# Sliding-window attention followed by a GELU feed-forward, on one core: loading and first product in smaller pieces, the first attention in another order, joined stores in the tail, value loads behind a wait

## The chip, the cores and the metric

The kernel runs on one core of one Trainium2 chip. Its engines work side by side and meet at semaphores: TensorE (PE, with its weight loads listed as PEld), VectorE (DVE), ScalarE (ACT), GpSimd (POOL) and SyncE (SP). SP issues most loads; ACT and POOL issue some DMAs too. All DMAs run on 16 DMA engines. The metric is the device time in microseconds of one execution, less being better.

## The reference

Two stages are computed, the second on the output of the first. All inputs and the output are fp32.

```python
# q, k, v: (8, 8, 576, 64): batch, heads, sequence, head dimension
scores = (1 / sqrt(64)) * q @ k.transpose(0, 1, 3, 2)
mask   = abs(pos[:, None] - pos[None, :]) <= 32           # a band of 65 keys for each query
attn   = softmax(where(mask, scores, -1e9))
x      = (attn @ v).transpose(0, 2, 1, 3).reshape(4608, 512)

h   = x @ w_in                                            # (512, 2048)
g   = 0.5 * h * (1 + tanh(sqrt(2 / pi) * (h + 0.044715 * h**3)))
out = g @ w_out                                           # (2048, 512) -> (4608, 512)
```

## The kernel before

**Stages.** The 4608 tokens of the second stage are nine tiles of 512 (`t` = 0 to 8), those of attention eight batches of 576 (`b` = 0 to 7). Before the loop stands a start-up: load batch 0, attention of batch 0, load and cast of `w_in`, and the first product of tile 0. Then stage `t` multiplies tile `t` with `w_in` (`ffn_in`, L456), applies GELU on ACT (L464), and multiplies with `w_out` while the attention of batch `t` + 1 is woven in between the matmuls by a table written by hand (`PLAN`, `PLAN_0`: "s" scores, "m" mask, "v" weigh with the values, "x" spread into `xT`). Tile 0 uses plain matmuls for the second product (`ffn_out_0`, L525), the others a Winograd form of 7 half-size products (`ffn_out`, L551).

**The order.** Nothing is scheduled by a planner: each engine and each queue takes its instructions in the order of the program text. An instruction waits for what it reads and for the buffer that it writes, and everything behind it on its engine waits with it.

**Loads and casts.** SP's queue holds, in this order: batch 0's q, k, tails and v; `w_in` in four column blocks of 512 (`load_w_in`, L192; block 0 in two loads, the others in one each); batch 1's q and k (L136); `w_out` (L196) in four blocks, the last in two loads, with batch 1's values between them; batch 2's q and k (L165, L167). Weights arrive as fp32 in a pool of five staging buffers and are cast to fp16 by `cast_w` (L201), chunk by chunk of 128 rows. Block 0 and block 1 of `w_in` are cast by POOL alone, the later blocks by DVE (chunks 0 and 1) and POOL (2 and 3).

**First attention.** Batch 0 is handled in four pairs of heads. For each pair q and k are cast to fp16 (`cast_early`, L264), transposed by PE (`trans_pair`, L293 and L295), copied out of PSUM by DVE (`trans_out`: QT at L300, KT at L301), multiplied to scores (`score`, L360), exponentiated on ACT (L370), masked by the band on DVE (`mask`, L376), weighed with the values (`weigh`: sums at L389, values at L395), inverted on ACT (`invert`, L408 and L409), and spread into `xT` by DVE (`spread`, L418). The values of a pair are cast by POOL (`cast_v`, L274) and then copied to a shifted place by DVE (`pair_v`, L182 and L183). `spin` (L227) issues PE work that nobody reads, to fill PE's waiting time. The tails are the last 64 positions of the sequence.

**Later batches.** From batch 2 on, q and k are cast by DVE (L321, L329) and transposed by DMA from SP's queue (`cast_and_turn`: QT at L324, KT in two halves at L331, KL at L336). Values are loaded as fp16 by POOL's queue (`load_v`: four loads at L175, a fifth at L177), each batch one stage ahead. In stage `t` ≥ 1 the loads of batch `t` + 2 stand in POOL's queue right where the plan weighs the tail of the batch before (`v-1`), ahead of that stage's stores; the loads of batch 2 stand earlier, in the first product of stage 1, behind a one-column POOL copy (L727) that waits for a GELU. The pair copies of V are two DMAs on SP at the end of the stage.

**Stores.** `store` (L515) writes 128 rows of a tile. Rows lie in the order (position modulo 4, position), so the rows are cut where that order jumps; in a tail of a batch this gives runs of 24 rows (16 for batch 0). In the last tile the stores alternate between SP and ACT; in the others they are on POOL.

Of the kernel before, what the change touches and what calls it, by code (L numbers as in the profile page):

```python
# [64 lines left out]
def kernel(  # L65
# [9 lines left out]
    nc = tc.nc  # L75
# [5 lines left out]
    NT = NTOK // 512  # L81
# [25 lines left out]

    load_table(exp_set)


    idn = const.tile([128, 128], FP16, name="idn")
    full = const.tile([128, 4, 56], FP16, name="full")
    ones = const.tile([128, 64], FP16, name="ones")
# [74 lines left out]
    def stage_w():  # L188
        return stage.tile([128, 4, 512], FP32, name="wst", tag="stage")

    def load_w_in(i, w, c0=0, c1=4):
        nc.sync.dma_start(w[:, c0:c1, :], w_in_v[:, c0:c1, 512 * i:512 * i + 512])  # L192
        return w
# [2 lines left out]
        nc.sync.dma_start(w[:, c0:c1, :], w_out_v[:, 4 * i + c0:4 * i + c1, :])  # L196
        return w

    def cast_w(w, dst, on_dve=2, cs=range(4), on_act=()):
        for c in cs:  # L200
            (nc.scalar.copy if c in on_act else nc.vector.tensor_copy if c < on_dve else nc.gpsimd.tensor_copy)(  # L201
                dst[:, c, :], w[:, c, :])

    qk, tails, vs, vtail = load_early(0)
# [7 lines left out]
    vs(2, 3)  # L212
    vs(4, 5)
    vs(6, 7)
    wi = [load_w_in(0, stage_w(), 0, 2)]
    load_w_in(0, wi[0], 2, 4)
    wi[1:] = [load_w_in(i, stage_w()) for i in range(1, 4)]


    idle = KTs[1][:, 0, 0:512]  # L220
    nc.vector.memset(idle, 0.0)
# [33 lines left out]
    QTs = {}  # L255
# [40 lines left out]
        if now:  # L296
            trans_out(b, pr, pt)

    def trans_out(b, pr, pt):
        nc.vector.tensor_copy(QTs[b][:, pr, :, 0:128], pt[:, 0:4, :])  # L300
        nc.vector.tensor_copy(  # L301
            KTs[b % 2][:, pr, :].rearrange("d (p j) -> d p j", j=4),
            pt[:, 4:8, :].rearrange("d j p -> d p j"))
# [5 lines left out]
    def bank16(i):  # L309
        return psM.tile([128, 8, 128], FP16, name="pt", tag=f"x{i}")  # L310
# [190 lines left out]
    out_v = out.rearrange("(b p j) f -> b j p f", b=B, j=4)  # L501
    pys = {}

    turn_about = [nc.sync, nc.scalar]

    def store(t, t4, yo, cols=slice(0, 512), eng=None):
        m = 0
        while m < 128:
            b, c = divmod(t * 512 + t4 * 128 + m, S)
            q0, n = (0, cut(b)) if c < 4 * cut(b) else (cut(b), 144 - cut(b))  # L510
            j, p = divmod(c - 4 * q0, n)
            e = min(n - p, 128 - m)
            if t == NT - 1 and eng is None:
                turn_about.reverse()
            (eng or turn_about[0] if t == NT - 1 else eng or nc.gpsimd).dma_start(  # L515
                out_v[b, j, q0 + p:q0 + p + e, cols], yo[m:m + e, cols])
            m += e

    later, unpaired = [], []

# [13 lines left out]
    def ffn_out(t, i):  # L534

        n, blk, f = i // 16, i // 8 % 2, i % 8
        a, w, new = WINO[n]
        end = t == NT - 1
        if i % 16 == 0 and new:
            pys[n % 2] = bank((1 + n) % 2)  # L540
            if end and n == 4:
                pys["apart"] = psO.tile([128, 512], FP32, name="py2", tag="O")
        py = pys[n % 2].rearrange("p (b c) -> p b c", b=2)
        apart = end and blk and n in (4, 6)
        if a[0] == "A":
            r0, c0 = 8 * (int(a[2]) - 1) + f, 256 * (int(a[1]) - 1) + 128 * blk
            lhsT = gTs[t][:, r0, c0:c0 + 128]
        else:
            lhsT = wino[a][:, f, 128 * blk:128 * blk + 128]
        one = end and n in (4, 6)  # L550
        nc.tensor.matmul(pys["apart"][:, 0:256] if apart else py[:, blk, :], lhsT,  # L551
                         wino[w][:, f, :], start=(new and i % (8 if one else 16) == 0),
                         stop=(i % (8 if one else 16) == (7 if one else 15)),
                         skip_group_check=True)
        if i % 16 < 15:
            return
        yo, left, right = wino["yo"], slice(0, 256), slice(256, 512)
        C11, C12, C21, C22 = (yo[:, r:r + 2, c] for r in (0, 2) for c in (left, right))

        M1, U2, U3 = C21, C12, C22  # L560
        if n == 0:
            nc.vector.tensor_copy(M1, py)
        elif n == 1:
            nc.vector.tensor_tensor(U2, py, M1, op=ALU.add)
        elif n == 2:
            nc.vector.tensor_copy(C11, py)
            if end:
                for x in range(2):
                    store(t, x, yo[:, x, :], left, nc.sync)
        elif n == 3:  # L570
            nc.vector.tensor_tensor(U3, py, M1, op=ALU.add)
        elif n == 4:
            if not end:
                nc.vector.tensor_tensor(C22, py, U3, op=ALU.add)
            else:
                for x, part in enumerate((py[:, 0, :], pys["apart"][:, 0:256])):
                    nc.vector.tensor_tensor(C22[:, x, :], part, U3[:, x, :], op=ALU.add)
                    store(t, 2 + x, yo[:, 2 + x, :], right)
        elif n == 5:
            nc.vector.tensor_tensor(C21, py, M1, op=ALU.add)  # L580
            for x in range(2):
                store(t, 2 + x, yo[:, 2 + x, :], left if end else slice(0, 512))

    def ffn_last(t):
        py = pys[0].rearrange("p (b c) -> p b c", b=2)
        yo, right = wino["yo"], slice(256, 512)
        for x in range(2):
            part = pys["apart"][:, 0:256] if x and t == NT - 1 else py[:, x, :]
            nc.vector.tensor_tensor(yo[:, x, right], part, yo[:, x, right], op=ALU.add)
            if t < NT - 1:  # L590
                store(t, x, yo[:, x, :])
            else:
                store(t, x, yo[:, x, :], right, nc.scalar if x else nc.sync)


    cast_open(0)
    cast_early(0, 0, (nc.vector, nc.gpsimd))
    trans_pair(0, 0, bank16(0))
    cast_tails(0, nc.vector)
    spin(3, 512)  # L600
    trans_tails(0, bank16(1))
    both = (nc.gpsimd, nc.gpsimd)
    cast_early(0, 1, both)
    cast_early(0, 2, both)
    cast_v(0, 0)
    cast_early(0, 3, both)
    cast_v(0, 1)
    cast_v(0, 2)
    cast_v(0, 3)
    cast_w(wi[0], w_in16[:, :, 0:512], 0, (0, 1))  # L610
    cast_w(wi[0], w_in16[:, :, 0:512], 0, (2, 3))


    qk, tails, vs, vtail = load_early(1)
    for h in range(0, H, 2):
        qk(h)
    wo = [load_w_out(0, stage_w())]

    def turn(g):
        pt = bank16(0)  # L620
        trans_pair(0, g, pt, now=False)
        return pt

    def weighed(g):
        o, d = weigh(0, g, other=(g % 2 == 0))
        ods[g] = (o, invert(0, g, o, d))

    def paired(g):
# [1 line left out]

    ods = {}
    score(0, 0, 0)
    spin(2, 512, 1)
    pt = turn(1)
    trans_out(0, 1, pt)
    mask(0, 0)
    spin(4, 512, 1)
    score(0, 1, 1)
    pt = turn(2)
    trans_out(0, 2, pt)  # L640
    cast_vt(0)
    mask(0, 1)
    spin(4, 512, 0)
    score(0, 2, 0)
    paired(0)
    spin(3, 512, 1)
    weighed(0)
    mask(0, 2)
    pt = turn(3)
    trans_out(0, 3, pt)  # L650
    spread(0, 0, *ods[0])
    spin(4, 512, 1)
    score(0, 3, 1)
    paired(1)
    spin(2, 512, 0)
    weighed(1)
    paired(2)
    mask(0, 3)
    weighed(2)
    spread(0, 1, *ods[1])  # L660
    ffn_in(0, 0, 0, 2)
    paired(3)
    spread(0, 2, *ods[2])
    weighed(3)
    for fc in (1, 2, 3):
        ffn_in(0, fc, 0, 2)
    for fc in range(4):
        ffn_in(0, fc, 2, 3)
    cast_w(wi[1], w_in16[:, :, 512:1024], 0)
    for fc in (4, 5):  # L670
        ffn_in(0, fc, 0, 3)
    spread(0, 3, *ods[3])
    for c in (2, 3):
        cast_w(wi[c], w_in16[:, :, 512 * c:512 * c + 512])
    wo += [load_w_out(1, stage_w()), load_w_out(2, stage_w())]
# [35 lines left out]
    for t in range(NT):  # L711
# [28 lines left out]
        for i in range(113 if t else 65):  # L740
            for act in plan.get(i, "").split():
# [14 lines left out]
                elif kind == "t":  # L756
                    trans_tails(1, bank16(1))
                elif kind == "c":
                    if g == 1:
                        B12 = combine_w()  # L760
                    combine(g, nc.vector)
                elif kind == "s":
                    score(*group(g), at)
                elif kind == "d":
                    pair_v(b, nc.vector.tensor_copy, slice(2 * g, 2 * g + 2))
                elif kind == "m":
                    mask(*group(g))
                elif kind == "v":
                    bb, gg = group(g)
                    o, d = weigh(bb, gg, at)  # L770
                    ods[g] = (o, invert(bb, gg, o, d))
                    if t and g < 0 and b + 1 < B:
                        load_v(b + 1)
                        unpaired.append(b + 1)
                    if t and g == (3 if att else -1):
                        load_table(gelu_set)
                else:
                    spread(*group(g), *ods[g])
# [1 line left out]
                pair_v(2, nc.vector.tensor_copy, slice(i // 10, i // 10 + 4))  # L780
                unpaired[:] = [3]
            if t == 0 and i in (61, 62):
                store(0, *later.pop(0), eng=nc.scalar)
            if t == 0 and i < 64:
                ffn_out_0(*ORDER_0[i])
            elif t and i < 112:
# [41 lines left out]
```

The softmax here doesn't subtract the row's maximum and nothing guards it: scores larger than these inputs give would overflow.

## Time and profile before

| | |
|---|---|
| median of 8 runs | 303.5 us (302.08 to 305.26) |
| the profiled execution's own time | 304.23 us |
| its span, from the first to the last instruction | 302.5 us |
| PE busy | 287.5 us (95%) |
| DVE, ACT, POOL busy | 194.6, 186.9, 105.2 us |
| HBM read and written | 36.70 MB, 9.44 MB |
| DMA packets | 116831, of which 97519 are under 512 B |

The profile is one execution, and its own time stands 0.73 us above the median. Times in the trace count from the first instruction. In lines of the timeline the columns are the start, the length, the engine, the source line, the operation with its tiles (out<-in) and shapes, the count of merged instructions, and in brackets the engine's idle time just before, with what ended it. "SPq" and "ACTq" are issues of DMAs by these engines. A wait for several things is put down to the one that came last.

The chain of work that ended last is 72% PE, 13% DMA and 10% SP's queue; its DMA and SP parts lie in the first 81 us.

### The profile page before, as it was taken

The numbers are of one execution on the slowest core, as the hardware profiler recorded it, in microseconds if no ns is written. First come the engines' busy times: TensorE is split into PE (matmuls) and PEld (weight loads), VectorE is DVE, ScalarE is ACT, GpSimd is POOL, SyncE is SP. The second block draws the span as 40 slices with busy tenths as digits, with TensorE's granted clock in tenths as the row PEclk, the third lists the DMA queues.
The fourth block names the chain that finished last, engine by engine and source line by source line (L and its number), as shares of the span: only waits on it lengthen the run. The fifth ranks groups of instructions, "written<-read, shape, count | busy, mean of one in ns | idle before, by whom it ended". The sixth has DMA issues, their size and how long they took to land.

```text
span 302.5 us, 7135 instructions
## 1 busy us (share of the span) xinstructions
PE 287.5 (95%) x2886; PEld 180.6 (60%) x2886; DVE 194.6 (64%) x429; ACT 186.9 (62%) x287; POOL 105.2 (35%) x160
## 2 busy tenths in 40 slices
PE   6888999998999999999999999999999999999993
PEld 2533544443785478547854785478547864784582
DVE  4782769959969566856685668566866635443442
ACT  1665567487656695669566856785668666606500
POOL 3655556356008500850085007600710070015000
PEclk9999999999999999999999999999999999999999
DMA  6999999999999999699979995999690031004013
GB/s 203 257 319 375 359 278 261 273 209 173 157 245 191 198 239 186 156 154 225 203 170 174 240 200 130 175 235 194 104 212 11 2 89 51 3 12 126 2 45 95
DMA packets 116831, 52.44 MB, mean 173 GB/s; under 512 B 97519, under 2 KB 109551, under 8 KB 116798
## 3 DMA queue, kind: packets, MB, share of 16 engines
q1 hardware_dynamic: 84233, 39.66, 60.0%
q0 software_dynamic: 31776, 11.41, 32.9%
q10 hardware_dynamic: 789, 0.92, 1.0%
q8 instruction: 22, 0.36, 0.6%
q14 instruction: 11, 0.09, 0.1%
HBM read 36.70 MB, written 9.44 MB: 153 GB/s over the span
## 4 chain that ended last, share of the span: by engine, by line
PE 72%; DMA 13%; SPq 10%; POOL 2%; issue 1%; DVE 1%; ACT 0%; DVEq 0%; POOLq 0%
PE mm L551 31%; PE mm L456 18%; PE ph L456 14%; DMA wst<-in_moe_w_in_dram 4%; DMA KT<-k 4%; DMA wst<-in_moe_w_out_dram 3%; PE ps_s L360 3%; SPq L145 2%; DMA qt<-in_q_dram 2%; PE ps_d L389 2%; SPq L167 2%; PE ps_o L395 2%; SPq L136 2%; POOL w_in L201 1%; SPq L150 1%
## 5 line engine op out<-in xcount | busy, mean ns | idle before, releaser
L456 PEld LDWEIGHTS <-w_in 128*128 128x128 f16 x576 | 56.1, 98 | 67.9 <-POOL w_in L201 3.4
L515 POOL DMA_DIRECT2D out_dram<-y x77 | 46.5, 612 | 112.4 <-DVE y L580 98.7
L456 PE MATMUL mm<-xT,w_in 128*128 128x512 f16 x320 | 78.4, 379 | 0.9 <-POOL w_in L201 0.8
L464 ACT ACTIVATE gT<-mm 128x512 f16<-128x512 f32 x80 | 47.6, 599 | 46.3 <-PE mm L456 45.5
L456 PE MATMUL ph<-xT,w_in 128*128 128x512 f16 x256 | 64.6, 379 | 1.1 <-POOL w_in L201 1.1
L499 DVE TENSOR_TENSOR s<-gT 128x512 f16<-128x512 f16 x64 | 26.9, 420 | 41.7 <-ACT gT L464 41.7
L551 PEld LDWEIGHTS <-s 128*128 128x128 f16 x512 | 49.6, 98 | 5.9
L370 ACT ACTIVATE pe<-ps_s 128x960 f16<-128x960 f32 (+1 forms) x32 | 30.5, 976 | 23.1 <-PE ps_s L360 23.0
L551 PE MATMUL mm<-t,s 128*128 128x256 f16 x376 | 44.7, 273 | 0.0
L464 ACT ACTIVATE gT<-ph 128x512 f16<-128x512 f32 x64 | 36.0, 602 | 10.1 <-PE ph L456 9.9
L551 PEld LDWEIGHTS <-gT 128*128 128x128 f16 x384 | 36.0, 98 | 6.6
L551 PE MATMUL mm<-w_out,gT 128*128 128x256 f16 x256 | 32.8, 273 | 0.0
L409 ACT ACTIVATE lt<-lt 128x480 f32<-128x480 f32 (+3 forms) x40 | 23.5, 587 | 1.3
L175 POOL DMA_DIRECT2D V<-in_v_dram x24 | 22.3, 951 | 1.1 <-PE mm L456 0.5
L90 ACT ACT_TABLE_LOAD x17 | 21.8, 1283 | 1.1 <-PEq L812 0.8
L408 ACT ACTIVATE lt<-ps_d 128x480 f32<-128x480 f32 (+2 forms) x29 | 16.0, 553 | 10.2 <-PE ps_d L389 6.2
L376 DVE TENSOR_TENSOR pe<-pe,band 128x960 f16<-128x960 f16 (+1 forms) x32 | 21.0, 674 | 1.1 <-ACT pe L370 1.0
L395 PEld LDWEIGHTS <-V 128*64 128x64 f16 x520 | 14.6, 111 | 4.4 <-DVE V L183 1.2
L551 PE MATMUL mm<-t,gT 128*128 128x256 f16 x128 | 16.3, 273 | 0.0
L360 PE MATMUL ps_s<-QT,KT 64*64 64x128 f16 (+3 forms) x576 | 13.2, 216 | 2.6 <-DMA KT<-k 1.9
L360 PEld LDWEIGHTS <-KT 64*64 64x64 f16 x576 | 9.6, 106 | 9.4 <-issue 4.6
L551 PE MATMUL mm<-w_out,s 128*128 128x256 f16 x120 | 14.4, 273 | 0.0
(90 smaller groups left out, 305.2 us busy)
## 6 DMA issues: line engine op xcount, KB each, us to landing
kr<-in_k_dram SPq DMA_DIRECT2D x32, 256.0 KB, 8.2
qr<-in_q_dram SPq DMA_DIRECT2D x6, 1024.0 KB, 7.9
wst<-in_moe_w_in_dram SPq DMA_DIRECT2D x3, 1024.0 KB
wst<-in_moe_w_out_dram SPq DMA_DIRECT2D x3, 1024.0 KB, 12.4
V<-in_v_dram POOLq DMA_DIRECT2D x24, 128.0 KB, 7.7
qr<-in_q_dram SPq DMA_DIRECT2D x8, 256.0 KB, 10.5
vr<-in_v_dram SPq DMA_DIRECT2D x16, 128.0 KB, 3.9
V<-V SPq DMA_DIRECT2D x5, 256.0 KB
```

The lines of the kernel that those rows point to most:

```text
L90: nc.scalar.add_instruction(mybir.InstLoadActFuncSet(name=nc.get_next_instruction_name(), act_func_set_id=which, ins=[], outs=[]))
L175: nc.gpsimd.dma_start(V[:, c, :, :], v[b, :, 128 * c:128 * c + 128, :].rearrange("h p d -> p h d"))
L360: nc.tensor.matmul(ps[64 * half:64 * half + 64, h, 4 * n * r:4 * n * r + 4 * n].rearrange("k (j p) -> k j p", j=4)[:, :, p0 - q0:p1 - q0], ...
L370: nc.scalar.activation(pe, ps[:, :, 0:w], AF.Exp, scale=SCALE)
L376: nc.vector.tensor_tensor(pe, pe, m.rearrange("k (o j) p -> k o j p", o=1).broadcast_to(list(pe.shape)), op=ALU.mult)
L395: nc.tensor.matmul(o[64 * h:64 * h + 64, cols].rearrange("d (j p) -> d j p", j=4)[:, :, p0 - q0:p1 - q0], Vs[b % 2][:, slot, 2 * pr + h, : ...
L409: nc.scalar.activation(lt[:, 0:n], lt[:, 0:n], AF.Exp, scale=-1.0)
L456: nc.tensor.matmul(ph, w_in16[:, dc, fc * 128:fc * 128 + 128], xT[:, dc, t * 512 % RING:t * 512 % RING + 512], start=(dc == 0), stop=(dc = ...
L464: nc.scalar.activation(gTs[t][:, fc, :], phs[fc], AF.Gelu_apprx_tanh)
L499: nc.vector.tensor_tensor(dst, x, y, op=op)
L515: (eng or turn_about[0] if t == NT - 1 else eng or nc.gpsimd).dma_start(out_v[b, j, q0 + p:q0 + p + e, cols], yo[m:m + e, cols])
L551: nc.tensor.matmul(pys["apart"][:, 0:256] if apart else py[:, blk, :], lhsT, wino[w][:, f, :], start=(new and i % (8 if one else 16) == 0) ...
```

## The change

It has five parts.

1. **Weights in halves.** Each of the four blocks of `w_in` is loaded by two DMAs in place of one (block 0 had two already). Block 1 is cast by DVE (chunks 0 and 2) and POOL (1 and 3) in place of POOL alone.
2. **First product chunk by chunk.** The first columns of the first product are computed for one chunk of the inner dimension after the other over four columns (then over two), and all of it stands behind the last weighing; before, some of it stood between the weighings.
3. **First attention reordered.** The q casts of pairs 1 and 2 go from POOL to DVE, the QT copies of pairs 0 and 2 from DVE to ACT; pair 0's KT copy stands behind the cast of the tails; the spins are other numbers at other places; pair 2's sums and values go to a score bank (`pair=1`); the casts of values and of block 0 stand later in the text, in the same order on POOL.
4. **Stores joined.** Where the cut runs are whole, up to four of them become one DMA with three dimensions (4 x 24 rows x columns). In the last tile, SP and ACT take fixed turns within each call.
5. **Value loads held.** In stages 1 to 5 a one-column POOL copy that reads KL (the last of the transposed keys) stands in front of the value loads of the next batch but one.

```diff
@@ loads of w_in
-    wi = [load_w_in(0, stage_w(), 0, 2)]
-    load_w_in(0, wi[0], 2, 4)
-    wi[1:] = [load_w_in(i, stage_w()) for i in range(1, 4)]
+    wi = []
+    for i in range(4):
+        wi.append(load_w_in(i, stage_w(), 0, 2))
+        load_w_in(i, wi[i], 2, 4)
@@ copies of the transposed pairs
-    def trans_out(b, pr, pt):
-        nc.vector.tensor_copy(QTs[b][:, pr, :, 0:128], pt[:, 0:4, :])
+    def trans_out(b, pr, pt, copy=nc.vector.tensor_copy):
+        copy(QTs[b][:, pr, :, 0:128], pt[:, 0:4, :])
@@ store
-    def store(t, t4, yo, cols=slice(0, 512), eng=None):
+    def store(t, t4, yo, cols=slice(0, 512), *engs):
...
             e = min(n - p, 128 - m)
-            if t == NT - 1 and eng is None:
-                turn_about.reverse()
-            (eng or turn_about[0] if t == NT - 1 else eng or nc.gpsimd).dma_start(
-                out_v[b, j, q0 + p:q0 + p + e, cols], yo[m:m + e, cols])
+            nj = 1 if p else max(1, min(4 - j, (128 - m) // n))
+            eng = engs[i % len(engs)] if engs else nc.gpsimd
+            if nj > 1:
+                e = nj * n
+                eng.dma_start(out_v[b, j:j + nj, q0:q0 + n, cols], yo[m:m + e, cols])
+            else:
+                eng.dma_start(out_v[b, j, q0 + p:q0 + p + e, cols], yo[m:m + e, cols])
             m += e
+            i += 1
@@ the last tile: x = 0 and 1
-                    store(t, 2 + x, yo[:, 2 + x, :], right)
+                    store(t, 2 + x, yo[:, 2 + x, :], right, nc.sync, nc.scalar)
...
-                store(t, 2 + x, yo[:, 2 + x, :], left if end else slice(0, 512))
+                store(t, 2 + x, yo[:, 2 + x, :], *((left, nc.sync, nc.scalar) if end else ()))
...
-                store(t, x, yo[:, x, :], right, nc.scalar if x else nc.sync)
+                store(t, x, yo[:, x, :], right, *((nc.scalar, nc.sync) if x else (nc.sync,)))
@@ start of the first attention
-    cast_early(0, 0, (nc.vector, nc.gpsimd))
-    trans_pair(0, 0, bank16(0))
+    split = (nc.vector, nc.gpsimd)
+    cast_early(0, 0, split)
+    pt = bank16(0)
+    trans_pair(0, 0, pt, now=False)
     cast_tails(0, nc.vector)
-    spin(3, 512)
+    trans_out(0, 0, pt, nc.scalar.copy)
     trans_tails(0, bank16(1))
...
@@ end of the first attention, first product
+    spin(2, 512, 0)
+    weighed(2, pair=1)
     spread(0, 1, *ods[1])
-    ffn_in(0, 0, 0, 2)
     paired(3)
+    weighed(3)
     spread(0, 2, *ods[2])
-    weighed(3)
-    for fc in (1, 2, 3):
-        ffn_in(0, fc, 0, 2)
-    for fc in range(4):
-        ffn_in(0, fc, 2, 3)
-    cast_w(wi[1], w_in16[:, :, 512:1024], 0)
-    for fc in (4, 5):
-        ffn_in(0, fc, 0, 3)
+    spin(3, 512, 0)
+    for dc in range(3):
+        for fc in range(4):
+            ffn_in(0, fc, dc, dc + 1)
     spread(0, 3, *ods[3])
+    cast_w(wi[1], w_in16[:, :, 512:1024], (0, 2))
+    for dc in range(3):
+        for fc in (4, 5):
+            ffn_in(0, fc, dc, dc + 1)
@@ value loads, stages 1 to 5
                     if t and g < 0 and b + 1 < B:
+                        nc.gpsimd.tensor_copy(after, KLs[b % 2][:, 3, 0:1])
                         load_v(b + 1)
```

## The prediction

> **What bounds the kernel now.** I read the table of windows first: the span cut into stages, each with its length, the busy time of each engine (instructions in brackets), the granted clock, the DMA share and the GB/s.
>
> ```profile
> 0.00:20.00 20.00, 15.44 (x193) 7.54 (x193) 13.77 (x33) 9.33 (x12) 10.23 (x22) 1.00 0.97 241
> 20.00:32.00 12.00, 10.67 (x62) 4.66 (x62) 4.56 (x9) 7.73 (x14) 7.02 (x12) 1.00 1.06 377
> 32.00:60.00 28.00, 25.77 (x293) 13.44 (x291) 22.84 (x42) 16.43 (x27) 13.95 (x19) 1.00 1.02 289
> 60.00:82.00 22.00, 20.15 (x192) 11.29 (x189) 17.76 (x40) 16.30 (x25) 10.38 (x13) 1.00 1.72 179
> 82.00:285.00 203.00, 202.86 (x2043) 132.74 (x2044) 129.08 (x295) 136.36 (x212) 63.66 (x97) 1.00 0.90 148
> 285.00:302.50 17.50, 12.60 (x114) 10.96 (x112) 6.59 (x13) 0.74 (x2) 0.00 (x0) 0.97 0.21 60
> ```
>
> The third column is PE. From 82 to 285 us PE idles 0.14 of 203 us: what the change frees there on other engines buys nothing. An edit can pay before 82, where the DMA share is about 1 or above (overlapping records count twice), and in the tail, where PE stops and stores remain. So I asked next who PE waits for (total, times, longest).
>
> ```profile
> PE ps_s L360 <- DMA KT<-k: 1.9, 2, 1.4
> PE ph L456 <- POOL w_in L201: 1.1, 3, 0.8
> PE mm L456 <- POOL w_in L201: 0.8, 2, 0.7
> PE mm L525 <- POOL w_out L201: 0.7, 2, 0.4
> ```
>
> The two w_in rows lie in the first product, the w_out row at the start of the second, the KT row in the stage t=1. Which of them end on the path is read from the timeline, in order of time:
>
> ```profile
> 24.38 0.39 PE L456 MATMUL ph<-xT,w_in 128*128 128x512 f16 x1 [0.77 <-POOL w_in L201]
> 38.91 1.61 POOL L201 CAST w_out<-wst 128x512 f16<-128x512 f32 x2 [2.79 <-DMA wst<-in_moe_w_out_dram]
> 39.82 0.38 PE L525 MATMUL mm<-w_out,gT 128*128 128x512 f16 x1 [0.36 <-POOL w_out L201]
> 66.17 1.79 DVE L329 CAST k<-kr 128x512 f16<-128x512 f32 x4 [3.33 <-DMA kr<-in_k_dram]
> 67.93 5.38 SPq L331 DMA_TRANSPOSE KT<-k  x2
> 69.28 4.00 POOL L175 DMA_DIRECT2D V<-in_v_dram  x4
> 75.78 0.62 PE L360 MATMUL ps_s<-QT,KT 64*64 64x96 f16 x32 [1.38 <-DMA KT<-k]
> 80.58 0.40 PE L360 MATMUL ps_s<-QT,KT 64*64 64x96 f16 x16 [0.47 <-DMA KT<-k]
> ```
>
> Time lost before 38.9 is not the path: the first w_out block lands there behind everything that SP queued earlier, POOL casts it, and PE waits 0.36 and then 0.37 us for the two casts. A PE that came earlier would wait longer. The same holds at 75.78: batch 2's keys land at 66.1 at the end of the load queue, are cast, transposed by DMA, and PE waits 1.38 us for the first half and 0.47 for the second. The tail:
>
> ```profile
> 291.37 7.99 SPq L515 DMA_DIRECT2D out_dram<-y  x13
> 293.73 5.17 ACTq L515 DMA_DIRECT2D out_dram<-y  x9
> 297.64 0.42 DVE L589 TENSOR_TENSOR y<-py,y 128x256 f32<-128x256 f32 x1 [0.45 <-PE py L551]
> 298.63 0.73 SPq L515 DMA_DIRECT2D out_dram<-y  x2
> ```
>
> The last sum ends at 298.06, but SP issues its last two stores at 298.63 and about 299.0, one sum late, because its queue is full; the span ends 3.1 us after 299.36.
>
> **Weights in halves.** SP issues eight loads for w_in in place of five, three more at 0.73 (five took 3.65): 2.2 us. Queued behind are batch 1's eight q and k loads, then w_out. The queue runs ahead of the data (w_in's second block is issued by 16.1, cast at 23.71) and the DMA engines are full at 1.06 from 20 to 32, so the bytes ahead of w_out, and its landing near 38.85, stay: 0. Were that cover gone, w_out would be up to 2.2 us late. The halves free block 1's casts, now two on DVE and two on POOL (0.59 and 0.57 each), from 23.71-26.0 to about 24.6 at the latest.
>
> **First attention.** DVE loses two query copies (0.42 each, to ACT, where the nearest row, a 128x512 copy, is 0.60) and gains two query casts (0.43 each, from POOL): nothing net, and DVE is the busiest of the helpers here. Pair 0's KT copy now stands behind the tails' cast, which waits for a load until 6.79; in exchange the query copies no longer stand ahead of the keys. ACT's copies queue in front of exponentials of 1.02 and behind them: pair 2's waits for the second one. Following the queues with these durations, the last spread ends near 23, as before (23.01); by orderings that I may have wrong, from 0.5 earlier to 1.5 later. Two spins fewer in all (28 for 30, 0.21 each) were wait filler.
>
> **First product chunk by chunk.** Before, 14 of its matmuls are done at 25.49, at the end of the waits for block 1, and ten more (24 make six columns) at 0.216 (eight take 1.73 in the chain) end at 27.65. After, they all stand behind the last weighing and three spins: the last weighing ends near 22.1, spins 0.65, so start near 22.8; 18 matmuls 3.9, to 26.7; the last chunk 6 x 0.216, to 28.0. So 0.3 us later, from 0.6 earlier to 1.8 later; the waits of 0.77 go and the deferral eats them. Up to 0.73 us of lateness disappears in the two waits for w_out and another 1.38 in the first wait for KT, in all 2.11, so this comes to 0, as does being early. Bounds: 0 and +0.3 when the worst of these and late q/k meet.
>
> **Value loads held.** A POOL copy of one column (0.19 in the row of the existing hold) now waits for KL before each of five batches' value loads. In t=1 the four loads of batch 3 leave POOL at 69.28, in the same microsecond as the second key transpose. From then to landing that transpose takes 11.26 us in the chain, the median of KT transposes being 7.5. Without the four loads, the second half should come at least 0.47 earlier: at 7.5 it is there at 76.8, before PE's 80.12. Gain 0.47. The first half, issued at 67.93, is past most of its way before those loads have descriptors; it still meets batch 2's loads of 64.5, which are not held. I take 0 there; bounds 0 and the full 1.38. Behind the hold on POOL stand the values themselves and then the stage's stores, which are 14 us away (POOL idles 13.8 for them); on SP, the pair copies of V. In later stages PE never waits for KT: 0 gain.
>
> **Stores joined.** Up to four runs of 24 rows become one. On POOL eight or nine issues for eleven, at 0.61 each, in idle time: 0. In the tail 16 issues for 22: SP has two pieces, then x=0's two, then one piece of the last sum, ACT one. SP after 296.61: four at 0.36 end at 298.05, so the last piece goes at 298.10, where the sum ends, in place of 299.01: 0.91 at most. ACT has 88 rows at 296.62, the joined piece, and the last 48 rows; the joined issue costs between one issue, 0.36, and four, 1.44, so ACT's last goes between 298.10 and 298.5. That leaves 0.5 to 0.9. No row shows a store of this form, so its transfer could also end last: between 0.9 gained and 0.3 lost. I take 0.6, near the issue rows, since the DMA share there is 0.21.
>
> The Trainium skill, page "DMA: Bandwidth & Descriptors", section "Why a DMA increments its semaphore by 16 and not by 1", speaks against this edit: a DMA is spread over the largest number of engines up to 16 that divides the slowest dimension on both sides. By it a joined piece (4 by 24 rows) runs on 4 engines and a 24-row piece on 12; the page's 27 GiB/s per engine makes an estimate of 0.8 us for 24 KB, on the four engines that the last pieces need too, and the tail would gain near 0. No row before has a joined store.
>
> **Sum.** The profiled execution took 304.23, 302.50 of it span and 1.73 around it. 302.50 - 0.47 - 0.6 = 301.43, with 1.73 it is 303.16, or 1.07 less. The median of the eight runs is 303.5, 0.73 below this execution; taking off 1.0 gives 302.5, which is 0.3%. Of no change a measurement of this kernel tells about 0.5%, 1.5 us, so the forecast itself lies inside.
>
> **Rivals.** B, more than forecast: the first half of the keys comes early too, as the values leave the rings, and the tail gains its full 0.91. 1.85 + 0.91 = 2.76, so 300.7. For it: the eight runs spread over 3.2 us, which 203 us with 0.14 us of idle PE are unlikely to make, so the waits for DMA may differ by this much between executions, and a hold may even them out. Against: the loads of 64.5 stay, and they are the ones in the first half's way.
>
> C, slower: the held values come too late for SP. In t=2 the loads left POOL at 98.97; KL is issued at 104.60 for 1.2 us, and lands by 106 to 111 (5.2 is the median of the nearest row, QT from qt). Four loads 3.62, the fifth 0.70, 7.7 to land: 118 to 123. SP issues the pair copies at 118.00 now and its next transpose at 125.24; the copies need 1.66 to issue, so up to 123.6 nothing changes. KT (7.5 after 128.24, 135.7) is needed near 137.2, which leaves 1.5 more: from values landing at 125.1 on, each stage pays. At half a microsecond in five stages it is 2.5 more, 306.0. Against: the bound is 2 us past the late end of my estimate, and the transposes themselves gain from the hold.
>
> D, it does not do what it says: halves and reorder are hidden, the second key half comes no earlier, and the joined pieces land as late as the split ones: 303.5.
>
> **Chances.** Forecast 0.50, of which 0.12 lies below 302.0 where the first keys gain part; B 0.28; C 0.16; D 0.06. Faster 0.12 + 0.28 = 0.40, within 0.38 + 0.06 = 0.44, slower 0.16. The forecast's own range is 301.6 to 303.8 (tail -0.9 to +0.3, keys -1.0 to 0). The range reaches down to B, 300.6, and up to D with the tail and the start each 0.3 late, 304.1, and 0.3 more, since the median of eight runs that spread over 3.2 us is uncertain by about that: 304.4. Outside lie C and little else.
>
> **What would show it.** Right: PE's wait for the second KT gone and about 1.4 left for the first; batch 3's value loads on POOL after 78; the last store issued near 298.1 minus the gain; PE at the first w_out matmul within 0.7 us of 39.82 and idle nowhere between 82 and 285. Wrong: w_out's cast off 38.91 by over 1 us, PE waits for KT or V after 100, or a span that ends more than 4 us after the last sum.

## The result, and the profile after

The changed kernel takes 309.79 us (median of 22 runs, 303.69 to 318.81) against 303.06 (62 runs, 301.51 to 306.98): slower. The ratio of the comparison is 1.0079, 95% interval 1.0048 to 1.0109; it leaves out executions over 1.5% above the fastest of their kernel, and of a kernel that spreads by 5% these are most, so the ratio of all medians, 1.022, stands beside it. The forecast was 302.5, range 300.6 to 304.4.

The profiled execution is the longest of the 22, 318.81 us, span 317.1, so it shows the harm at its largest. The table of windows, with the columns of the one before (third column PE busy; after POOL the granted clock, the DMA share, GB/s):

```profile
0.00:20.00 20.00, 14.57 (x169) 7.13 (x169) 12.13 (x29) 8.55 (x11) 7.67 (x19) 0.91 0.99 244
60.00:82.00 22.00, 18.21 (x139) 9.22 (x138) 15.73 (x36) 15.33 (x23) 6.73 (x11) 0.95 1.37 193
82.00:285.00 203.00, 196.62 (x2035) 130.91 (x2034) 126.44 (x286) 128.85 (x198) 54.28 (x80) 0.97 0.97 143
302.50:317.10 14.60, 10.06 (x93) 8.77 (x90) 5.12 (x10) 0.00 (x0) 0.00 (x0) 0.94 0.25 72
```

From 82 to 285 us PE, which idled 0.14 us before, now idles 6.38, and its clock is 0.97. Over the whole span PE is busy 293.69 us against 287.49 (the sum of the six rows before), 6.20 more for slower matmuls, and idle 23.41 against 15.01, 8.40 more: together the 14.6 us by which the two spans differ. The largest wait of PE, and the only one over 0.3 us after 60 us, has one releaser (total, times, longest):

```profile
PE ps_s L359 <- DMA KT<-k: 10.0, 3, 4.3
```

It was 1.9 us in two waits. The three lie in the stages t=1 (3.79 us, at 75.0), t=3 (1.97, at 141.4) and t=5. The timeline around the last:

```profile
193.16 0.47 SPq L181 DMA_DIRECT2D V<-V  x1
193.68 0.59 SPq L182 DMA_DIRECT2D V<-V  x1
194.37 7.07 SPq L323 DMA_TRANSPOSE QT<-q  x1
195.37 0.82 POOL L515 DMA_DIRECT2D out_dram<-y  x1
201.53 7.42 SPq L330 DMA_TRANSPOSE KT<-k  x2
210.28 1.01 PE L359 MATMUL ps_s<-QT,KT 64*64 64x96 f16 x32 [4.27 <-DMA KT<-k]
```

L515 is the joined store of tile 4, one microsecond behind the query transpose of batch 6. That transpose lands at 209.56, 15.19 us after its issue; the same one took 8.40 before. The two rows of V ahead of it are the pair copies, 448 KB, which land 4.2 and 4.6 us behind the transpose's issue. They stand there because of the hold (e4 below); in the kernel before they went out 3.7 to 7.7 us ahead of the query transpose, for instance 7.24 ahead of that of batch 4:

```profile
118.00 1.02 SPq L182 DMA_DIRECT2D V<-V  x1
125.24 2.90 SPq L324 DMA_TRANSPOSE QT<-q  x1
```

The joined store, with its time from issue to landing:

```profile
out_dram<-y POOLq DMA_DIRECT2D x1, 192.0 KB, 14.0
```

The joined store of 192 KB is under way for 14.0 us. In the kernel before, the four pieces of 48 KB that it replaces took 5.4 to 6.3 us each, and the last of them landed 7.6 us after the first was issued (187.54). The start is as expected or nearly, the tail in part:

```profile
38.50 1.41 POOL L200 CAST w_out<-wst 128x512 f16<-128x512 f32 x2 [2.83 <-DMA wst<-in_moe_w_out_dram]
40.70 1.90 PE L527 MATMUL mm<-w_out,gT 128*128 128x512 f16 x8
78.79 0.62 PE L359 MATMUL ps_s<-QT,KT 64*64 64x96 f16 x32 [3.79 <-DMA KT<-k]
312.60 0.42 DVE L591 TENSOR_TENSOR y<-py,y 128x256 f32<-128x256 f32 x1 [0.45 <-PE py L553]
313.05 0.33 ACTq L517 DMA_DIRECT2D out_dram<-y  x1
306.33 7.47 SPq L517 DMA_DIRECT2D out_dram<-y  x11
```

w_out is cast 0.41 earlier than before, the second product starts 0.88 later. ACT's last store goes out 0.03 us after the last sum ends at 313.02. SP's last goes out at 313.48, 0.46 after that sum, where SP's two went 0.57 and 0.95 after it before. It lands last of all, 3.07 us after the sum; before, the last landing came 2.77 us after it. The span ends 4.50 us after the last matmul, 4.92 before.

### The profile page after: what moved, and what is told of

It reads as the page before. It is cut to its first block, busy times and chain, and to the rows that moved or that the text cites. A ratio compares the mean times of both kernels' runs of the same rounds, so it can differ in the third digit from the quotient of the medians.

```text
span 317.1 us, 7117 instructions
## 1 busy us (share of the span) xinstructions
PE 293.7 (93%) x2884; PEld 183.9 (58%) x2884; DVE 194.3 (61%) x431; ACT 187.9 (59%) x289; POOL 93.8 (30%) x146
## 4 chain that ended last, share of the span: by engine, by line
PE 68%; DMA 17%; SPq 11%; POOL 1%; issue 1%; DVE 1%; ACT 0%; POOLq 0%
PE mm L553 32%; PE mm L455 15%; PE ph L455 12%; DMA KT<-k 9%; DMA wst<-in_moe_w_in_dram 3%; DMA wst<-in_moe_w_out_dram 3%; SPq L166 3%; PE ps_s L359 3%; SPq L144 3%; PE ps_d L388 2%; PE ps_o L394 2%; DMA qt<-in_q_dram 2%; SPq L135 1%; SPq L149 1%; SPq L191 1%
## 5 line engine op out<-in xcount | busy, mean ns | idle before, releaser
L517 POOL DMA_DIRECT2D out_dram<-y x55 | 32.9, 608 | 94.5 <-DVE y L582 87.3
L553 PEld LDWEIGHTS <-s 128*128 128x128 f16 x512 | 50.7, 100 | 7.1
L553 PE MATMUL mm<-t,s 128*128 128x256 f16 x376 | 46.6, 279 | 0.0
L553 PEld LDWEIGHTS <-gT 128*128 128x128 f16 x384 | 37.6, 102 | 8.1
L553 PE MATMUL mm<-w_out,gT 128*128 128x256 f16 x256 | 36.4, 293 | 0.0
L774 POOL COPY after<-KL 128x1 f16<-128x1 f16 x5 | 1.2, 244 | 63.7 <-DMA KL<-kt 63.7
```

Of the source, the lines that this page charges most:

```text
L517: eng.dma_start(out_v[b, j, q0 + p:q0 + p + e, cols], yo[m:m + e, cols])
```

## The experiments

Two theories grew out of the first runs, and e5 to e17 call them by letters. T: the joined store itself delays the transposes that are queued with it, because it lies on few DMA engines. V: joined stores are fewer issues on POOL, so the value loads behind them leave sooner and come among the transposes. Times are medians; the ratio stands against the kernel before on the same chip.

**e1: the changed kernel without joins.**

```diff
-            nj = 1 if p else max(1, min(4 - j, (128 - m) // n))
+            nj = 1
```

> The changed kernel with every run of rows stored by a DMA of its own again (the turns of SP and ACT in the tail stay). Theory J (a joined store of 4 x 24 rows sits on few DMA engines, runs beside the query and key transposes of the next batch and makes them land late): the waits of PE for KT after 100 us (2.0 and 4.3 in the profile after) go to 0, QT transposes land within 10 us of their issue, the median comes down from 309.8 to 302.5-304. Theory H (the held value loads are late and block SP's queue): the waits stay, the median stays above 306. Theory S (the start-up makes the loads late): the wait in t=1 stays near 3.8, the later ones go only if they came from J.

303.74 us, 1.001 (0.9968 to 1.0052). The joins are all of the loss; the new start, the hold and the fixed turns in the tail come to nothing that can be told. One KT wait of 2.14 us is left after 90 us, in t=6. There the query transpose takes 14.00 us, with no joined store near it, but with the pair copies of V issued 1.30 and 0.78 us ahead of it.

**e2: the changed kernel without the hold.**

```diff
-                        nc.gpsimd.tensor_copy(after, KLs[b % 2][:, 3, 0:1])
```

> The changed kernel without the POOL copy that holds the value loads. J: the waits of PE for KT after 100 us stay or grow, since values come on top of the joined stores: 308-314. H: they go, median 302.5-304, the pair copies of V are issued by SP some 8 us earlier again (near 118 in t=2 where they are at 126.7 after).

321.06 us, 1.0595 (1.0501 to 1.0689), KT waits of 13.5 us. Beside joined stores the hold is worth 11 us; with the old start it is 6 (e3 and e15 below).

**e3: the kernel before with the joined stores and the turns alone**

```diff
+            nj = 1 if p else max(1, min(4 - j, (128 - m) // n))
...
+            if nj > 1:
+                e = nj * n
+                eng.dma_start(out_v[b, j:j + nj, q0:q0 + n, cols], yo[m:m + e, cols])
```

> The kernel before with only the joined stores and the tail's turns. J: waits of PE for KT in t=3 to t=5 of 1-4 us each, 306-312. H and S: no wait after 100, tail 0 to 0.9 less, 302-303.5.

320.4 us, 1.055 (1.0489 to 1.061). One edit, priced at 0 outside the tail, costs 16 us: the title of this document puts the joined stores in the tail, but one stands in each of the tiles 1 to 7. Its waits of PE:

```profile
PE ps_s L360 <- DMA KT<-k: 10.6, 3, 3.8
```

They lie in the stages 2, 3 and 5, each behind a joined store of four pieces, that of tile 1, 2 or 4, issued within 1.5 us of a query transpose. The value loads leave POOL 2.1 to 2.2 us after that transpose there, 4.1 to 4.2 in the kernel before.

**e4: the kernel before with the hold alone**

```diff
+                        nc.gpsimd.tensor_copy(after, KLs[b % 2][:, 3, 0:1])
                         load_v(b + 1)
```

> The kernel before with only the hold of the value loads. J: no PE wait after 100, the second KT wait in t=1 gone, 302.3-303.3. H: SP's pair copies 5-9 us later, QT transposes behind them, PE waits for KT of 0.5-4 us in several stages, 305-310.

304.13 us, 0.9978 (0.9931 to 1.0025). The second KT wait of t=1 is gone, the first is 1.18 us. From t=2 on the query transposes take 7.97 to 11.12 us, for 6.72 to 8.78 before: the hold puts the pair copies only 1.0 to 4.5 us ahead of them. Without joined stores PE waits for none of them in this trace.

**e5: joined stores issued after the transposes have landed**

```diff
+                    late.append((to, fr))
...
                 cast_and_turn(b)
+                if late:
+                    nc.gpsimd.tensor_copy(after, KLs[b % 2][:, 3, 0:1])
+                for to, fr in late:
+                    nc.gpsimd.dma_start(to, fr)
```

> The kernel before with the joined stores of the third experiment, but the joined store of each of tiles 1 to 5 (one a tile) is issued on POOL only after the last key transpose of the next batch has landed; all else, the number of its bytes and of its issues too, is that of the third experiment (320.4 us against 304 or so for before). Theory T (a joined store lies on four DMA engines, and the transposes that are queued at the same time on all of them have to take turns with it there): 305 us (303 to 308), no PE wait for KT above 1.5 us after 90 us, query transposes back to 7 to 10 us from issue to landing. Rival P (a joined store is slow by itself, or dear for POOL, wherever it stands): 315 us or more, since nothing about the store is changed but its time.

311.63 us, 1.0245 (1.0181 to 1.031). No KT wait over 0.3 us and the first key halves land 3.6 to 7.4 us after their issue: the part on the transposes came true. The time did not: the late store keeps the sums' tile `yo`, and PE waits 3.35 and 1.31 us for DVE, which waits for it. That wait was not in the expectation; the run says nothing on P.

**e6: joined stores on SP's queue**

```diff
-            eng = engs[i % len(engs)] if engs else nc.gpsimd
+            eng = engs[i % len(engs)] if engs else nc.sync if nj > 1 else nc.gpsimd
```

> The kernel before with the joined stores, those of the steady tiles issued on SP's queue in place of POOL's, so that store and transposes go through one queue in the order of their issue. Theory T as to the four engines: 316 us (310 to 324), the same rows still lie on four engines ahead of the transposes. Rival Q (it is POOL's queue, its way of making the transfer or the sharing between two queues): 304 us (302 to 307), KT waits of under 1.5 us.

336.96 us, 1.1072 (1.0994 to 1.115), more than either theory said.

```profile
PE ps_s L360 <- DMA KT<-k: 26.3, 5, 6.2
```

It is not POOL's queue as such. With a store less on POOL the value loads leave 0.1 to 1.6 us after the query transpose, so the run mixes T and V. On SP's queue the landing marks of a joined store can be counted: five for one of four pieces, three for one of two; in the tails a plain one of 24 rows has 13.

**e7: joined stores of half a row.** Columns 0 to 255 of the pieces joined, 256 to 511 plain, a store a piece.

> The kernel before with joined stores of half a row: columns 0 to 255 of the pieces go in the joined store, columns 256 to 511 in one plain store a piece (so up to five issues for four pieces). Theory T: half the bytes on the four engines; in the third experiment the first key half landed 4.6 us later after the queries' issue than before (15.4 for 10.8) and PE waited 3.4 to 3.8, so 1.0 of it was cushion; half the delay leaves waits of 1 to 2 us at three places, 308 us (305 to 312). Rival P (a joined store costs as such, whatever its size): 318 us or more; rival N (the number of issues helped, their bytes not): 304.

303.67 us, 1.0035 (0.9999 to 1.007), no KT wait of 0.4 us or more after 60 us. T's 308 was wrong; but the five issues also hold the value loads back to 4.7 us and more after the transposes. This is what led to V.

**e8: at most two pieces to a joined store**

> The kernel before with at most two pieces to a joined store in the steady tiles: two stores of two pieces where the third experiment had one of four. Theory T, if both lie on the same two engines: twice the rows on each, 322 us or more, KT waits above 4 us; if they lie on different engines: as the third experiment, 318 to 321. Rival F (only the join of four pieces is slow; the two tiles that had a joined store of two pieces in the third experiment showed no KT wait): 304 us (302 to 307).

318.18 us (311.25 to 318.84, 4 runs; no ratio), KT waits of 2.42, 4.06 and 3.14 us: F is out, and T's branch of different engines fits. The value loads leave 3.2 to 3.3 us after the query transposes.

**e9: two joined stores of half a row each**

```diff
+                for half in (slice(0, 256), slice(256, 512)) if t < NT - 1 else (cols,):
+                    eng.dma_start(out_v[b, j:j + nj, q0:q0 + n, half], yo[m:m + e, half])
```

> The kernel before with the joined stores of the third experiment, each cut by columns into two joined stores of half a row (two issues for four pieces). The whole bytes lie on the same engines, in packets half as large. Theory L (the load on the four engines: 24 rows of 2 KB on each, 48 KB; half of it did no harm in the run with half rows): as the third experiment, 318 us (312 to 324), KT waits of 2.5 us or more after the query transposes of tiles 2, 3 and 5. Rival S (packets of two whole rows, 4 KB, that the transposes' packets of 256 B stand behind): 304 us (302 to 307), waits under 1.5 us.

313.76 us, 1.0339 (1.0269 to 1.0408), waits of 2.14, 3.73 and 2.03 us: rather less than L's. The run does not decide on S, because the edit did not make the packets smaller: from 90 to 280 us the trace has 1364 packets of 4096 bytes on POOL's queue and none of 1024, as e3's has. Nor is it shown whether the two halves lie on the same engines. S falls by e10 and e16 below: their packets are of 4096 bytes alike, joined or plain, and only the joined ones do much harm.

**e10: one joined store, that of tile 2, and the tail's**

```diff
+            nj = 1 if p or t not in (2, NT - 1) else max(1, min(4 - j, (128 - m) // n))
```

> The kernel before with one joined store only, that of tile 2 (four pieces of 24 rows, 129.48 us in the third experiment's trace), and the last tile's. Theory T (each joined store that lies beside the query transposes costs its own wait and the slow clock behind it; the third experiment has three such waits and lost 16 us): 308 us (306 to 311), one KT wait of 2.5 to 4.5 us near 140 us and none elsewhere after 90. Rival (the waits feed each other, so that a single one is taken up by the slack of the next tile): 304 us.

310.4 us, 1.0233 (1.0177 to 1.0289). One store of 192 KB, with the value loads that it brings forward (2.2 us after the query transpose, for 4.1), costs 7.1 us. The windows of its trace show where they go:

```profile
82.00:136.92 54.92, 54.92 (x539) 35.03 (x536) 37.98 (x91) 37.16 (x59) 20.57 (x28) 1.00 1.32 189
136.92:141.11 4.19, 0.00 (x1) 0.01 (x2) 1.52 (x4) 1.48 (x2) 0.00 (x0) 0.91 1.51 120
141.11:151.00 9.89, 9.89 (x133) 7.53 (x134) 3.86 (x7) 5.02 (x8) 0.70 (x1) 0.69 1.37 237
```

PE waits 4.19 us for KT, then works 9.89 us at a granted clock of 0.69, which loses 0.31 x 9.89 = 3.1: together 7.3. A wait of this length is paid nearly twice. The Trainium skill, page "TensorE: Matmul & The Clock Gate", section "Part 1: The HAM clock gate (the "warmup" mystery)", says that the clock falls to half after an idle window of about 3.4 us and comes back after as long a busy one. Here the granted clock is 0.50 for twice such a window, from 140.39 to 147.22, of which 6.11 us fall into the work behind the wait (3.1 / 0.5). The wait need not be as long as the page's window either: in the changed kernel 3.41 us at 0.50 (144.57 to 147.98) follow a wait of 1.97. Over all traces here, after 60 us, every wait of PE of 3 us or more was followed by such a stretch, and six of the eight between 1.9 and 3.

**e11: joined stores in all tiles but 1, 2 and 4**

> The kernel before with joined stores in all tiles but 1, 2 and 4, the three whose store went out within 2 us of a query transpose and was followed by a KT wait. Theory T: the four joined stores that are left lie after the query transposes' issue by over 2 us or have no transpose beside them at all (tiles 6 and 7), so 303.5 us (302 to 306) and no KT wait above 1.5 us. Rival P (joined stores cost wherever they stand): four sevenths of the 16 us, 312 us.

304.08 us, 1.002 (0.9983 to 1.0057), KT waits of 0.2 us in all after 82 us. A joined store costs nothing that can be told where it goes out 2.09 us behind the query transpose (tile 3), 1.43 us ahead of it (tile 5) or where there is none (6 and 7). The expectation has tile 5's behind the transpose, which is a misreading. The two beside a transpose are of two pieces, 96 KB, so the run does not tell place and size apart; of four pieces it has only tile 6's and the last tile's, with no transpose.

**e12: the hold, and joins and turns in the last tile alone**

> The kernel before with the hold of the value loads and with the joined stores and queue turns in the last tile alone, where no transpose is left. If the hold takes the second KT wait (0.47 us) and the tail's end after the last matmul is 0.3 to 0.5 us shorter (4.4 to 4.9 us in the runs with joined stores against 4.9 and 5.0 in those before it): 302.3 us, ratio 0.997 (0.993 to 1.001). Rival: the four-engine piece of the last tile ends later than the pieces it replaces: 303.5 us or more.

302.9 us, 1.0006 (0.9975 to 1.0038). No gain that can be told, and no better version found.

**e13: plain stores, value loads early.** The short runs of the tile stand behind the value loads; those of tile 5 are left out.

```diff
                         load_v(b + 1)
+                        for to, fr in late:
+                            nc.gpsimd.dma_start(to, fr)
```

> The kernel before with every store plain, but in tiles 1 to 5 POOL issues the short whole runs of 24 (tile 1: 16) rows only behind the value loads of the next batch but one, so that those loads leave POOL about 2 us after the query transpose in place of 4.1 us. Theory V (the joined stores did harm because POOL had fewer issues in front of the value loads, so that these came among the transposes): 318 us (311 to 323), KT waits of 2.5 us or more in the tiles where the loads come 2 us after the query transpose, with no joined store in any of them. Theory T (the joined store's four engines): 304 us (302 to 307), no KT wait above 1.5 us after 90 us.

325.57 us, 1.0704 (1.0622 to 1.0785), but for another reason than V's:

```profile
PE mm L558 <- DVE y L571: 14.5, 4, 4.3
PE ps_s L360 <- DMA KT<-k: 1.5, 2, 0.9
```

The stores behind the fifth value load keep `yo` again, four waits of 3.1 to 4.3 us. The loads, now 1.4 us after the query transpose (2.1 in one stage), cause KT waits of only 0.6 and 0.9. As the time is spoiled, these waits are what the run tells, and they speak for early loads alone being a small matter; but the short stores, too, are gone from beside the transposes.

**e14: joined stores, value loads put back by three copies on POOL**

```diff
+                        for _ in range(3):
+                            nc.gpsimd.tensor_copy(scratch, scratch)
                         load_v(b + 1)
```

> The kernel before with the joined stores of the third experiment, and on POOL, ahead of each batch's value loads, three copies of a 128x512 tile onto itself that nobody reads, about as long as the three issues that the join saved (0.6 us each), so that the loads leave POOL about 4 us after the query transpose as before. Theory V: 304 us (302 to 308), no KT wait above 1.5 us after 90 us. Theory T: 318 us (312 to 322), three waits as in the third experiment, since the joined stores are where they were.

310.1 us, 1.0224 (1.0165 to 1.0283): between the two.

```profile
PE ps_s L362 <- DMA KT<-k: 4.9, 3, 2.5
```

With the loads at 4.1 to 5.0 us the same joined stores still cause waits of 1.80, 2.54 and 0.53 us. So both are true in part, and each makes the other worse.

**e15: joined stores and the hold, old start**

> The kernel before with the joined stores and the hold of the value loads, that is the changed kernel with the old start. Theory V: the loads are away from the transposes, so nothing is left, 304 us (302 to 307), no KT wait above 1.5 us after 90 us. Theory T: the joined store itself delays the transposes, as for the changed kernel, 309 us (306 to 314), query transposes of 12 us and more and KT waits of 2 to 4 us in tiles 3 and 5. If both are true in part, this run measures T's part.

314.37 us, 1.0367 (1.0312 to 1.0422); waits of 5.89 us at 136.4 and 2.40 at 204.6, where the query transposes take 17.21 and 13.18 us. The value loads are out of the way, 16 to 22 us behind the transposes, yet the loss, 11 us, is more than e14's 7. The hold has brought something else: in these two stages the pair copies of V go out 2.45 and 1.20 us ahead of the query transpose and land up to 5.1 us behind its issue, where in e14 they went 7.43 and 6.69 ahead. So this run measures T with the pair copies, and e14 is the cleaner measure of T.

**e16 and e17: the same bytes in one issue, but as a plain run of rows**, without and with the hold.

```diff
-                eng.dma_start(out_v[b, j:j + nj, q0:q0 + n, cols], yo[m:m + e, cols])
+                to = out_v[b, j:j + nj, q0:q0 + n, cols] if t == NT - 1 else out_v[B - 1, 3, 0:e, cols]
+                eng.dma_start(to, yo[m:m + e, cols])
```

> The kernel of the third experiment, but each steady joined store writes its 96 (64, 48) rows as one plain run of rows, with the same 8 KB from row to row, into rows of the last batch that a later tile writes again, so the rows that it should have written stay unwritten. The same bytes, one issue at the same place, the value loads as early as in the third experiment; only the form is plain, and plain runs of 96 to 120 rows stand in every tile already. Theory T (the form of the join, four engines, does the harm; the earlier loads only add to it): 305.5 us (303 to 309), KT waits under 1.2 us each, as for plain stores with early loads. Theory I (any one large store at that place with early loads does it): 317 us (312 to 322), three waits of 3 us and more.

> The same plain run of rows in place of each steady joined store (the rows that it should have written stay unwritten), and the hold of the value loads. Beside the joined stores with the hold (314.4 us, waits of 5.9 and 2.4 us) only the form differs. Theory T: 304 us (302 to 307), no KT wait above 1.5 us after 90 us. Theory H (the hold itself does it once POOL has fewer stores, by the pair copies of V that come beside the next tile's stores): 312 us (309 to 316), waits of 2 us and more.

e16: 307.26 us, 1.0117 (1.0034 to 1.0201), KT waits of 2.5 us in all, the longest 1.64. e17: 305.65 us, 1.0055 (1.0009 to 1.01), no KT wait of 0.3 us or more. Against e3 (1.055) and e15 (1.0367) only the form of one store a tile differs, and with it the rows that it writes. Stretch 122 to 142 us of e10 and of e16, where both have one store of 192 KB 0.06 us after the query transpose, and value loads 2.1 to 2.2 us after it:

```profile
out_dram<-y POOLq DMA_DIRECT2D x1, 192.0 KB, 9.0
KT<-k SPq DMA_TRANSPOSE x2, 11.8
```

```profile
out_dram<-y POOLq DMA_DIRECT2D x1, 192.0 KB, 5.2
KT<-k SPq DMA_TRANSPOSE x2, 10.1
```

The first pair is the joined form, the second the plain one: the store lands in 5.2 us in place of 9.0, the query transpose in 10.17 in place of 13.30. A late landing of the store is not by itself the harm: in e17 the plain store of that place took 9.8 us, the query transpose 10.37, and no wait came. The four runs make a square: joined form alone 7 us (e14), earlier loads alone 4 (e16), both 16 (e3), neither 0 (the kernel before). The form is the larger part, and the two together cost more than their sum.

## Why the prediction was wrong

**Stores joined: the step that failed.** "On POOL eight or nine issues for eleven, at 0.61 each, in idle time: 0." It priced what POOL does and not what it sends. It measured 16 us in e3, by two ways that the step left out. First, the joined transfer beside the transposes: 9.0 us under way in e10 and 14.0 in the changed kernel, and the query transpose beside it 4.5 and 6.8 us longer than before (13.30 for 8.78, 15.19 for 8.40). Second, POOL's issues were no idle filler: in the kernel before they were what kept the value loads until 4.1 us after the query transpose, so POOL's queue should have been followed on to the loads. Waits of 3 to 4 us then count nearly double through the clock.

In the changed kernel the hold shuts the second way: the held loads leave 13 to 19 us after the query transpose. It opens a third, the pair copies beside the transposes. With the hold and plain stores (e1) the transpose that took 15.19 us took 11.33, so of the 6.8 us about 3 go with the hold and 4 with the join.

The rule of the skill that the prediction quoted for the tail (page "DMA: Bandwidth & Descriptors", section "Why a DMA increments its semaphore by 16 and not by 1") held in the landing marks where they can be counted: by it a joined piece is on 4 engines and a 24-row piece on 12, and the tails show one mark more than that, 5 in the changed kernel and 13 in the kernel before (e6's joined stores on SP have 5 as well). On POOL's queue every store shows 16 marks. There the starts of the packets speak for the rule: in tile 6 of e3, with no transpose in flight, the joined store's packets start four at a time (four from 261.29 to 261.36, four from 261.52 to 261.58), where the plain pieces of e10's tile 6 start twelve at a time (252.46 to 252.55). How a few-engine store makes the transposes late is not shown further than that. The error was to weigh the rule at the tail's quiet 0.21 DMA share and not from 82 us on, at 0.90.

**Tail.** Forecast 0.6, from 0.9 gained to 0.3 lost; measured 0.4 between the last matmul and the end, in one execution. In e3 and e12, with the same tail, it is 4.86 and 4.90 us for 4.92, so 0.6 was too much, and the estimate near 0, which the prediction worked out from the skill's rule, came closer. ACT's last store goes with the last sum, as foreseen; SP's does not. The prediction had it at the sum's end by issues of 0.36 us; the issue in front of it takes 0.64, and it goes 0.46 late.

**Value loads held.** The second KT wait of t=1 went, in e4 as in the changed kernel, whose batch 3 loads leave POOL at 81.04, after 78 as named. "I take 0" for the first half held in e4 (1.18 for 1.38). In the changed kernel's profile it is 3.79, with no joined store near; e1, with the same start and hold, shows 0.20. Why one execution pays it stays open, as does the changed kernel's wide spread. "In later stages PE never waits for KT: 0 gain" was right for the kernel before and wrong for the changed one, where the hold is worth 11 us (e2).

**Weights in halves, first attention, first product.** The landing of w_out hardly moved (its cast starts at 38.50 for 38.91), and the second product began 0.88 late, just beyond the 0.7 named; e1 shows that with the rest it comes to 0.

**Rivals and signs.** The two signs named for "wrong" that came were PE waits for KT after 100 us and the span's end 4.04 us (317.06 - 313.02) after the last sum. The second was badly chosen: in the kernel before the span ended 4.46 us after its last sum. Rival C had the right side and a part of the mechanism: it had the hold's values coming late for SP's pair copies. They do come later, but e4 shows no cost of that alone; C priced it at half a microsecond in five stages, and what the copies did was to add to the harm of the joins. What its chance of 0.16 lacked was a rival for the joins outside the tail. Why e15, without the new start, is slower (314.4) than the changed kernel (309.8) was not tried.

## What to carry to other kernels

Before joining DMAs to save issues, ask what is in flight beside them: price the transfer by its shape, not only its issue, and keep a slow-landing form away from transfers that somebody waits for. Follow the queue past the removed instructions too: what stood behind them starts sooner, and that may be the wrong moment. A hold moves traffic rather than taking it away: look also at what the held work releases in its turn. An idle matrix engine of over 3 us, often of 2, is to be counted with the slow clock behind it.

## What was not expected of the hardware

A store of 96 rows of 2 KB took 5.2 us from issue to landing as a plain run and 9.0 us as four joined pieces, at the same place beside a query transpose (e16, e10); with no transpose beside it, in the changed kernel's tile 6, the joined form took 4.6 us. With the hold, and so with the pair copies of V in flight, it was 9.8 as a plain run and 14.8 as joined pieces (e17, e15). Half the bytes in the joined form showed no harm (e7), though the loads were later there too. After a wait of 4.19 us the granted clock was 0.69 over the next 9.89 us; after one of 1.97 us it was 0.50 for 3.41.
